# First-half sums kept in tiles of the split sums and of outputs; a third tile each for queries and values, one more of 64-bit words, two more of 32-bit words

## The chip, the cores and the metric

The kernel runs on 1 core of one Trainium2 chip. The metric is the device time of one execution in microseconds (us). A core has five engines that run side by side, each through its own list of instructions in a fixed order: TensorE (PE, matrix products, with PEld for its weight loads), VectorE (DVE), ScalarE (ACT), GpSimd (POOL) and SyncE (SP, which in this kernel issues nearly all DMAs, written SPq in the profile). An instruction whose data or tile is not ready holds up all that stand behind it on its engine.

## The reference

An attention over 4 batches of 12 heads, then two feed-forward blocks on its output:

```python
# q, k, v: (4, 12, 448, 64)
q_n, k_n = rmsnorm(q, g_q), rmsnorm(k, g_k)
attn = softmax(q_n @ k_n.T / sqrt(64));  x = (attn @ v), heads side by side   # 1792 x 768
h = x @ moe_w_in            # 768 -> 2048
g = relu(h) ** 2
x = g @ moe_w_out           # 2048 -> 768
a, b = x @ moe2_w1, x @ moe2_w2          # 768 -> 1024
out = ((a * b) @ moe2_w3) @ moe2_w_out   # 1024 -> 1024 -> 768
```

The weights arrive as 64-bit floating-point numbers, the rest as 32-bit ones.

## The kernel before

**Products in three parts.** Each 32-bit operand of a feed-forward product is split into a high part (`split_hi`, a copy on ACT) and the rest (`split_lo`, a subtraction on POOL or DVE). `mm3` (L262 to L264) sums high x high, high x rest and rest x high.

**Units of weights.** The weights come as units of 128 x 384 or 128 x 512 numbers, in the order of the list `units`. A 64-bit unit passes through five steps: `load_next` brings it by DMA into a `raw64` tile (L180, 4 tiles); `words` turns its high word on ACT (L194) and its low word on POOL (L200, or ACT L198) into parts of a 32-bit number; `join` (L207, DVE) puts them together in a `raw` tile (6 tiles); `store` writes that to memory for the later batches (L215); `split_hi` and `split_lo` make the `hl` pair that the products read (both at helper lines, L106 and L114). A `raw64` tile is free again after its `join`, a `raw` tile after its `split_lo` and its `store`. `advance` writes these steps a few units ahead of use, by `LOAD64_AHEAD`, `WORD_AHEAD` and the like. There are 120 units of 64 bits; all others are loaded as 32-bit numbers straight into `raw` tiles (L183).

**Stages.** While the 12 heads of batch 0 are worked on, the product of w3 and w_out of the second block is made (`gen_w3o`, units of w3t and wo). While the heads of batch 1 are worked on, the two blocks of batch 0 run (`gen_moe`), with the 64-bit units of w_in, w_out, w1 and w2. Batches 2 and 3, and the end, run with stored 32-bit units. The main loop over heads writes one head's attention in pieces (scores L524 and L525, their maximum `nb` L526 and L527, exponentials `p` L543, transposes L570, products with v L622) and between them `fill` steps of the feed-forward products. From head 12 on the exponentials go through a DMA on SP (`pw<-p`, L549) before their transposes.

**Order.** A scheduler then orders each engine's instructions: an instruction is placed as soon as its inputs, its engine and a free tile of its pool are there by the scheduler's own reckoning, earlier ones of the program first. So the number of tiles of a pool decides how far ahead an engine's list runs.

**First-half sums.** The 2048-wide layer is done in two halves. `keep(e)` (L340) copies the sums of the first half of `w_out` into an `acc` tile on ACT, 6 in all; `add(e)` (L346) adds those of the second half on DVE and splits the sum into an `x2` pair (6 tiles).

Of the kernel before, what the change touches and what calls it, by code (L numbers as in the profile page):

```python
# [8 lines left out]
F32 = mybir.dt.float32  # L9
F32R = mybir.dt.float32r  # L10
U16 = mybir.dt.uint16
U32 = mybir.dt.uint32
# [17 lines left out]
def attention_moe_kernel(  # L30
# [16 lines left out]
    B, P, H, C, D = q_nat.shape  # L47
    S = P * C
# [26 lines left out]
    JOIN_AHEAD = 2  # L75
    WORD_AHEAD = 3
    LOAD32_AHEAD = 3
    LOAD64_AHEAD = 5

    const = ctx.enter_context(tc.tile_pool(name="const", bufs=1))  # L80
    xp = ctx.enter_context(tc.tile_pool(name="x", bufs=8))
    actp = ctx.enter_context(tc.tile_pool(name="act", bufs=8))
    x2p = ctx.enter_context(tc.tile_pool(name="x2", bufs=6))
    accp = ctx.enter_context(tc.tile_pool(name="acc", bufs=6))
    rawp = ctx.enter_context(tc.tile_pool(name="raw", bufs=6))
    hlp = ctx.enter_context(tc.tile_pool(name="hl", bufs=4))
    t2 = ctx.enter_context(tc.tile_pool(name="t2", bufs=2))
    t1 = ctx.enter_context(tc.tile_pool(name="t1", bufs=1))
    t3 = ctx.enter_context(tc.tile_pool(name="t3", bufs=3))
# [81 lines left out]
    def is64(i):  # L171
        return units[i][0].dtype != F32

    def load_next():
        i = pos["load"]
        src = units[i][0]
        n = src.shape[-1]
        if is64(i):
            t = t3.tile([128, 512, 2], U32, name="raw64", tag="raw64", bufs=4)
            nc.sync.dma_start(out=t[:, :n, :], in_=src.bitcast(U32).rearrange("p (n t) -> p n t", t=2))  # L180
        else:
            t = rawp.tile([128, 512], F32, name="raw", tag="raw")
            nc.sync.dma_start(out=t[:, :n], in_=src)  # L183
        raws[i] = t
        pos["load"] += 1
# [134 lines left out]
    def gen_moe(b):  # L320
        u = U0 + b * (2 * NFC + 4 * NE + 4 * NJ + 2 * NE)
        x = [xs.pop((b, i)) for i in range(KX)]
        acc = [None] * NE
        x2 = [None] * NE
        for half in range(2):
# [11 lines left out]

            def keep(e):
                def f(ps):
                    acc[e] = accp.tile([128, S], F32, name="acc", tag="acc")  # L340
                    copy_on("a", acc[e], ps)
                return f

# [65 lines left out]
    def load_head(h):  # L409
        if not (0 <= h < NH):  # L410
            return
        b, hh = divmod(h, H)
        t = t2.tile([128, S], F32, name="qt", tag="qt")
        nc.sync.dma_start(out=t, in_=q_t[b, hh])
        qts[h] = t

    def load_v(h):
        if not (0 <= h < NH):
            return
        b, hh = divmod(h, H)  # L420
        t = t2.tile([128, C, D], F32, name="v", tag="v")
        nc.sync.dma_start(out=t, in_=v_in[b, hh])
        vs[h] = t

# [343 lines left out]
```

## Time and profile before

| | |
|---|---|
| median of 3 runs | 1235.23 us (1233.96 to 1238.2) |
| the profiled execution: its time, its span | 1234.55 us, 1232.8 us |
| mean granted TensorE clock | 0.991 |
| busy, us: PE, DVE, ACT, POOL | 1160.9, 709.7, 728.5, 781.3 |
| DMA | 207.63 MB, mean 168 GB/s |

The span is the time from the first to the last instruction. Busy times are unions of an engine's instructions. In rows of instructions, `out<-in` are tiles by the program's names, x is a count, and the bracket gives the engine's idle time before the instruction and what ended it.

### The profile page before, as it was taken

Reading aid. Unit: us, or ns where it says so; the run is one execution under the profiler, and the core shown is the slowest. Engines: PE = TensorE matmul, PEld = TensorE weight load, DVE = VectorE, ACT = ScalarE, POOL = GpSimd, SP = SyncE. Lnnn points to the kernel's source line nnn. Section 1 sums busy time; section 2 is a strip of 40 time slices with the busy share of each in tenths; the row PEclk is TensorE's granted clock in tenths of the full one; section 3 lists DMA queues with packets and bytes.
Section 4 is the critical chain, followed back from the end, with each engine's and each line's share of the span. In section 5 each row is a group of like instructions: output and inputs, shape, how many; then the busy total and the mean of one; then the engine's idle time right before and its main releaser. Section 6 shows DMA issues by size and latency. Waiting matters only on the chain.

```text
span 1232.8 us, 18950 instructions
## 1 busy us (share of the span) xinstructions
PE 1160.9 (94%) x6192; PEld 1049.3 (85%) x6192; DVE 709.7 (58%) x1314; ACT 728.5 (59%) x1553; POOL 781.3 (63%) x772
## 2 busy tenths in 40 slices
PE   3789999998989899999999999999999999999998
PEld 2578888886878789998998998999999999999998
DVE  6699879768978774646567555655664421012100
ACT  5889876767657565656645555656545554343342
POOL 5875534655676655766776764856766556678673
PEclk9999999999998999999999999999999999999999
DMA  7774557888888755555535455544544443333342
GB/s 218 244 238 151 165 146 226 276 283 264 251 264 257 234 180 179 146 148 145 151 118 161 139 169 158 143 142 127 154 123 120 138 138 113 107 116 102 104 125 75
DMA packets 111347, 207.63 MB, mean 168 GB/s; under 512 B 12208, under 2 KB 66704, under 8 KB 111248
## 3 DMA queue, kind: packets, MB, share of 16 engines
q1 hardware_dynamic: 107792, 200.92, 54.0%
q10 hardware_dynamic: 3456, 5.51, 1.2%
q8 instruction: 49, 0.80, 0.3%
q14 instruction: 50, 0.41, 0.1%
HBM read 149.95 MB, written 27.53 MB: 144 GB/s over the span
## 4 chain that ended last, share of the span: by engine, by line
PE 60%; DMA 4%; DVE 2%; POOL 2%; ACT 1%; issue 1%; SPq 0%; DVEq 0%; POOLq 0%; ACTq 0%
PE mm L262 17%; PE mm L263 17%; PE mm L264 17%; PE kv L622 3%; PE pt L570 3%; DMA raw<-w 2%; DMA pw<-p 2%; PE sc L525 1%; PE sc L524 1%; POOL hl L114 1%; DVE raw L207 1%; PE kv L508 1%; PE mm L611 0%; ACT p L543 0%; POOL x L114 0%
## 5 line engine op out<-in xcount | busy, mean ns | idle before, releaser
L114 POOL TENSOR_TENSOR hl<-raw,hl 128x384 fp32r<-128x384 f32 (+1 forms) x383 | 446.4, 1169 | 258.5 <-ACT hl L106 253.3
L106 ACT ACTIVATE hl<-raw 128x384 fp32r<-128x384 f32 (+1 forms) x416 | 233.7, 564 | 147.6 <-PE mm L264 85.6
L263 PE MATMUL mm<-x,hl 128*128 128x448 f32 (+1 forms) x832 | 306.2, 368 | 8.6 <-POOL x L114 8.6
L262 PE MATMUL mm<-x,hl 128*128 128x448 f32 (+1 forms) x832 | 310.5, 373 | 3.8 <-ACT x L106 1.8
L264 PE MATMUL mm<-x,hl 128*128 128x448 f32 (+1 forms) x832 | 305.7, 367 | 4.5 <-POOL hl L114 2.6
L263 PE MATMUL mm<-act,hl 128*128 128x448 f32 (+1 forms) x640 | 234.4, 366 | 3.3 <-POOL act L114 3.2
L262 PE MATMUL mm<-act,hl 128*128 128x448 f32 (+1 forms) x640 | 236.9, 370 | 0.0
L264 PE MATMUL mm<-act,hl 128*128 128x448 f32 (+1 forms) x640 | 233.6, 365 | 0.7 <-DVE hl L114 0.7
L543 ACT ACTIVATE p<-sc,nb,rr 112x448 f32<-112x448 f32 x192 | 137.4, 719 | 86.4 <-DVE nb L527 83.0
L263 PEld LDWEIGHTS mm<-x,hl 128*128 128x128 f32 x832 | 158.1, 190 | 22.1 <-POOL x L114 10.2
L264 PEld LDWEIGHTS mm<-x,hl 128*128 128x128 f32 x832 | 158.2, 190 | 19.0 <-POOL hl L114 4.0
L262 PEld LDWEIGHTS mm<-x,hl 128*128 128x128 f32 x832 | 157.9, 190 | 18.5 <-ACT x L106 3.3
L526 DVE TENSOR_REDUCE nb<-sc 112x1 f32<-112x448 f32 x192 | 113.1, 615 | 35.6 <-PE sc L525 34.3
L263 PEld LDWEIGHTS mm<-act,hl 128*128 128x128 f32 x640 | 121.0, 189 | 14.3 <-POOL act L114 4.8
L264 PEld LDWEIGHTS mm<-act,hl 128*128 128x128 f32 x640 | 120.9, 189 | 10.6 <-DVE hl L114 1.1
L262 PEld LDWEIGHTS mm<-act,hl 128*128 128x128 f32 x640 | 121.0, 189 | 9.4
L114 DVE TENSOR_TENSOR ptr<-pt,ptr 128x448 fp32r<-128x448 f32 x144 | 87.1, 619 | 72.0 <-ACT ptr L106 71.4
L200 POOL TENSOR_SCALAR raw<-raw 128x384 uint32<-128x384 uint16 (+1 forms) x110 | 82.1, 747 | 73.0 <-DMA raw<-w_in 18.8
L207 DVE SCALAR_TENSOR_TENSOR raw<-raw 128x384 uint32<-128x384 uint32 (+1 forms) x120 | 84.8, 711 | 39.8 <-POOL hl L114 25.2
L194 ACT ACTIVATE raw<-raw 128x384 f32<-128x384 f32 (+1 forms) x120 | 70.5, 597 | 53.9 <-DMA raw<-w 18.0
L114 POOL TENSOR_TENSOR act<-gf,act 128x448 fp32r<-128x448 f32 x80 | 97.4, 1218 | 7.2 <-DVE gf L334 3.0
L334 DVE TENSOR_TENSOR gf<-mm,r 128x448 f32<-128x448 f32 x64 | 39.8, 621 | 94.4 <-ACT r L330 93.9
(82 smaller groups left out, 1588.7 us busy)
## 6 DMA issues: line engine op xcount, KB each, us to landing
pw<-p SPq DMA_DIRECT2D x72, 392.0 KB, 4.3
raw<-f_in SPq DMA_DIRECT2D x96, 192.0 KB, 2.4
raw<-f_out SPq DMA_DIRECT2D x72, 256.0 KB, 2.7
raw<-f SPq DMA_DIRECT2D x96, 192.0 KB, 2.4
raw<-w_in SPq DMA_DIRECT2D x32, 384.0 KB, 4.5
raw<-w_out SPq DMA_DIRECT2D x24, 512.0 KB, 6.1
raw<-w SPq DMA_DIRECT2D x32, 384.0 KB, 4.9
raw<-w3o SPq DMA_DIRECT2D x48, 256.0 KB, 2.7
```

The source lines that it names most:

```text
L106: nc.scalar.activation(out=out, in_=in_, func=AF.Copy)
L114: e.tensor_tensor(out=out, in0=in0, in1=in1, op=ALU.subtract)
L194: nc.scalar.activation(out=hi, in_=hi, func=AF.Prelu, scale=2.0**-112, alpha=-(2.0**32))
L200: nc.gpsimd.tensor_scalar(out=t[:, :n, 0], in0=low, scalar1=2.0**-13, scalar2=2.0**-14 - 0.5, op0=ALU.mult, op1=ALU.add)
L207: nc.vector.scalar_tensor_tensor(out=f[:, :n].bitcast(U32), in0=t[:, :n, 1], scalar=3, in1=t[:, :n, 0], op0=ALU.logical_shift_left, op1=AL ...
L262: nc.tensor.matmul(ps, w[:, 0, wk, :], x[0], start=(i == 0), stop=False)
L263: nc.tensor.matmul(ps, w[:, 0, wk, :], x[1], start=False, stop=False)
L264: nc.tensor.matmul(ps, w[:, 1, wk, :], x[0], start=False, stop=(i == last))
L334: nc.vector.tensor_tensor(out=gf, in0=ps, in1=r, op=ALU.mult)
L526: nc.vector.tensor_reduce(out=nb[:, j:j + 1], in_=o[j], axis=AX.X, op=ALU.max, negate=True)
L543: nc.scalar.activation(out=p, in_=o[j], func=AF.Exp, scale=d["rq"][:, c:c + 1], bias=nb[:, j:j + 1], accum_out=sm[:, i, c:c + 1],)
L570: nc.tensor.transpose(to[:kn, c * P:(c + 1) * P], d["p"][c][:, k0:k0 + kn], one)
```

## The change

The pool of `acc` tiles goes. The first-half sums 0 to 3 lie in two `x2` tiles, two sums in each, and the sums 4 and 5 in the two `osb` tiles, which the outputs use as well. The room is given to one more `raw64` tile (5), two more `raw` tiles (8), and a third tile each for `qt` and `v`. `LOAD64_AHEAD` is 6 in place of 5, so a 64-bit load is written one unit earlier.

```diff
--- before.py
+++ after.py
@@ -75,14 +75,13 @@
     JOIN_AHEAD = 2
     WORD_AHEAD = 3
     LOAD32_AHEAD = 3
-    LOAD64_AHEAD = 5
+    LOAD64_AHEAD = 6
 
     const = ctx.enter_context(tc.tile_pool(name="const", bufs=1))
     xp = ctx.enter_context(tc.tile_pool(name="x", bufs=8))
     actp = ctx.enter_context(tc.tile_pool(name="act", bufs=8))
     x2p = ctx.enter_context(tc.tile_pool(name="x2", bufs=6))
-    accp = ctx.enter_context(tc.tile_pool(name="acc", bufs=6))
-    rawp = ctx.enter_context(tc.tile_pool(name="raw", bufs=6))
+    rawp = ctx.enter_context(tc.tile_pool(name="raw", bufs=8))
     hlp = ctx.enter_context(tc.tile_pool(name="hl", bufs=4))
     t2 = ctx.enter_context(tc.tile_pool(name="t2", bufs=2))
     t1 = ctx.enter_context(tc.tile_pool(name="t1", bufs=1))
@@ -176,7 +175,7 @@
         src = units[i][0]
         n = src.shape[-1]
         if is64(i):
-            t = t3.tile([128, 512, 2], U32, name="raw64", tag="raw64", bufs=4)
+            t = t3.tile([128, 512, 2], U32, name="raw64", tag="raw64", bufs=5)
             nc.sync.dma_start(out=t[:, :n, :], in_=src.bitcast(U32).rearrange("p (n t) -> p n t", t=2))
         else:
             t = rawp.tile([128, 512], F32, name="raw", tag="raw")
@@ -337,7 +336,11 @@
 
             def keep(e):
                 def f(ps):
-                    acc[e] = accp.tile([128, S], F32, name="acc", tag="acc")
+                    if e >= 4:
+                        acc[e] = t2.tile([128, S], F32, name="osb", tag="osb")
+                    elif e % 2 == 0:
+                        pair = x2p.tile([128, 2, S], F32, name="acc", tag="x2")
+                        acc[e], acc[e + 1] = pair[:, 0, :], pair[:, 1, :]
                     copy_on("a", acc[e], ps)
                 return f
 
@@ -410,7 +413,7 @@
         if not (0 <= h < NH):
             return
         b, hh = divmod(h, H)
-        t = t2.tile([128, S], F32, name="qt", tag="qt")
+        t = t2.tile([128, S], F32, name="qt", tag="qt", bufs=3)
         nc.sync.dma_start(out=t, in_=q_t[b, hh])
         qts[h] = t
 
@@ -418,7 +421,7 @@
         if not (0 <= h < NH):
             return
         b, hh = divmod(h, H)
-        t = t2.tile([128, C, D], F32, name="v", tag="v")
+        t = t2.tile([128, C, D], F32, name="v", tag="v", bufs=3)
         nc.sync.dma_start(out=t, in_=v_in[b, hh])
         vs[h] = t
 
```

No instruction is added or taken away. The lists of the engines change in the following places. Line numbers of the change are 3 higher behind its `keep`, and 1 lower ahead of it.

DVE in the second half of the stage of batch 0's blocks, from the two transposes `ptr` ahead of a head's last scores to their maxima `nb`; the joins are the rows `raw<-raw64`, and a tile's number in the change is two or three lower than in the kernel before. Before:

```order
L114 TENSOR_TENSOR ptr_2969<-pt_2964,ptr_2969 128x448
L207 SCALAR_TENSOR_TENSOR raw_3094<-raw64_2980 128x512
L114 TENSOR_TENSOR hl_2987<-raw_2935,hl_2987 128x512
L207 SCALAR_TENSOR_TENSOR raw_3119<-raw64_3009 128x512
L207 SCALAR_TENSOR_TENSOR raw_3151<-raw64_3055 128x512
L114 TENSOR_TENSOR khl_3458<-kx_3456,khl_3458 112x4x64
L114 TENSOR_TENSOR ptr_3040<-pt_3035,ptr_3040 128x448
L114 TENSOR_TENSOR pte_3047<-pt_3042,pte_3047 64x448
L207 SCALAR_TENSOR_TENSOR raw_3215<-raw64_3089 128x384
L207 SCALAR_TENSOR_TENSOR raw_3257<-raw64_3114 128x384
L526 TENSOR_REDUCE nb_3079<-sc_3080 112x1
L526 TENSOR_REDUCE nb_3079<-sc_3084 112x1
```

The same place of the change:

```order
L113 TENSOR_TENSOR ptr_2968<-pt_2963,ptr_2968 128x448
L206 SCALAR_TENSOR_TENSOR raw_3212<-raw64_3053 128x384
L113 TENSOR_TENSOR hl_2986<-raw_2934,hl_2986 128x512
L206 SCALAR_TENSOR_TENSOR raw_3254<-raw64_3087 128x384
L206 SCALAR_TENSOR_TENSOR raw_3284<-raw64_3112 128x384
L113 TENSOR_TENSOR khl_3455<-kx_3453,khl_3455 112x4x64
L113 TENSOR_TENSOR ptr_3039<-pt_3034,ptr_3039 128x448
L113 TENSOR_TENSOR pte_3046<-pt_3041,pte_3046 64x448
L206 SCALAR_TENSOR_TENSOR raw_3306<-raw64_3144 128x384
L529 TENSOR_REDUCE nb_3077<-sc_3078 112x1
L529 TENSOR_REDUCE nb_3077<-sc_3082 112x1
```

Between the same attention rows stand joins of later units: where the join into raw_3151 stood right ahead of `khl`, now stands that into raw_3284 (raw_3287 of before), and raw_3306 (3309 of before) stands ahead of the maxima in place of raw_3257.

POOL at the same place, with the low words (`raw64<-raw64`) of the units that DVE joins there. The number of a `raw64` tile is that of its place of loading, which lies one unit earlier in the change: by the join rows, raw64_3008 is now the unit of raw_3149, which was raw64_3055 before. Before:

```order
L200 TENSOR_SCALAR raw64_2980<-raw64_2980 128x512
L114 TENSOR_TENSOR x_2954<-xf_2580,x_2954 128x448
L200 TENSOR_SCALAR raw64_3009<-raw64_3009 128x512
L114 TENSOR_TENSOR hl_3016<-raw_2985,hl_3016 128x512
L200 TENSOR_SCALAR raw64_3055<-raw64_3055 128x512
L108 TENSOR_SCALAR khl_3458<-kx_3456 112x4x64
L480 TENSOR_TENSOR kx_3769<-kn_2168,rr_2585 112x256
```

Of the change:

```order
L199 TENSOR_SCALAR raw64_3087<-raw64_3087 128x384
L113 TENSOR_TENSOR x_2953<-xf_2579,x_2953 128x448
L199 TENSOR_SCALAR raw64_3112<-raw64_3112 128x384
L113 TENSOR_TENSOR hl_3015<-raw_2984,hl_3015 128x512
L199 TENSOR_SCALAR raw64_3144<-raw64_3144 128x384
L107 TENSOR_SCALAR khl_3455<-kx_3453 112x4x64
L483 TENSOR_TENSOR kx_3766<-kn_2167,rr_2584 112x256
```

Before, the low word of the unit that DVE joins ahead of `khl` (raw64_3055) was POOL's last row ahead of its own `khl`; now that unit's low word (raw64_3112) stands two rows earlier, and the last one (raw64_3144) is joined only behind DVE's `khl`, `ptr` and `pte`.

SP from the third to the fourth DMA of exponentials (`pw<-p`) of batch 1; `raw<-w_in` and `raw<-w_out` are loads of 64-bit units. Before:

```order
L549 DMA pw<-p 112x896
L180 DMA raw_2626<-w_in 128x768
L215 DMA f_in<-raw 128x384
L180 DMA raw_2645<-w_out 128x1024
L215 DMA f_in<-raw 128x384
L180 DMA raw_2692<-w_out 128x1024
L414 DMA qt<-q_t 128x448
L549 DMA pw<-p 112x896
```

Of the change:

```order
L552 DMA pw<-p 112x896
L214 DMA f_in<-raw 128x384
L179 DMA raw_2691<-w_out 128x1024
L214 DMA f_in<-raw 128x384
L179 DMA raw_2715<-w_out 128x1024
L214 DMA f_in<-raw 128x384
L179 DMA raw_2763<-w_out 128x1024
L214 DMA f_in<-raw 128x384
L417 DMA qt<-q_t 128x448
L552 DMA pw<-p 112x896
```

There are three unit loads between the two DMAs in both lists, but they are three units further on: the first two loads of w_out, which stood here, are issued ahead of the third `pw<-p`. Of the DMAs of exponentials 6 to 20, each stands behind three or four more unit loads than before.

PE near the start, from the second scores of head 1 on (the rows `mm` are products of `gen_w3o`, three for each wo unit, which is an `act` tile here). Before:

```order
L525 MATMUL sc_446<-kt_353,ql_203 112x448
L570 MATMUL pt_482<-ident_103,p_417 128x112
L570 MATMUL pt_489<-ident_103,p_417 128x112
L262 MATMUL mm_226<-act_306,hl_290 128x384
L263 MATMUL mm_226<-act_306,hl_290 128x384
L264 MATMUL mm_226<-act_306,hl_290 128x384
L524 MATMUL sc_450<-kt_353,qh_202 112x448
L525 MATMUL sc_450<-kt_353,ql_203 112x448
L570 MATMUL pt_482<-ident_103,p_417 128x112
L570 MATMUL pt_489<-ident_103,p_417 128x112
L262 MATMUL mm_226<-act_318,hl_290 128x384
```

Of the change:

```order
L573 MATMUL pt_481<-ident_100,p_416 128x112
L573 MATMUL pt_488<-ident_100,p_416 128x112
L261 MATMUL mm_223<-act_305,hl_289 128x384
L262 MATMUL mm_223<-act_305,hl_289 128x384
L263 MATMUL mm_223<-act_305,hl_289 128x384
L261 MATMUL mm_223<-act_317,hl_289 128x384
L262 MATMUL mm_223<-act_317,hl_289 128x384
L263 MATMUL mm_223<-act_317,hl_289 128x384
L261 MATMUL mm_223<-act_332,hl_289 128x384
L262 MATMUL mm_223<-act_332,hl_289 128x384
L263 MATMUL mm_223<-act_332,hl_289 128x384
L527 MATMUL sc_449<-kt_352,qh_199 112x448
```

Two groups of three products have moved ahead of the scores sc_449 (sc_450 of before). Further on, 63 in place of 48 products stand ahead of the first scores of head 2; from that head's second half on the counts differ by 6 at most, and from head 11 on by none. The order of the products and the attention on PE is then the same.

## Rows read from the trace of the kernel before

**Rows 1.** Busy time by stretch: us, each engine (count), PEclk, DMA share, GB/s.

```profile
0.00:60.00 60.00, 30.32 (x115) 21.55 (x116) 39.29 (x89) 39.63 (x82) 42.36 (x52) 0.97 0.74 231
60.00:210.00 150.00, 138.66 (x838) 124.58 (x837) 136.36 (x279) 123.59 (x270) 80.10 (x98) 1.00 0.61 182
210.00:450.00 240.00, 214.57 (x1109) 189.91 (x1108) 190.86 (x338) 153.94 (x335) 150.47 (x161) 0.96 0.81 256
450.00:1232.80 782.80, 777.40 (x4135) 713.25 (x4133) 343.13 (x612) 411.31 (x869) 508.38 (x463) 1.00 0.45 134
```

**Rows 2.** Waits of PE from 210 to 450 us: total, times, longest.

```profile
PE sc L524 <- ACT p L543: 8.8, 8, 2.4
PE pt L570 <- DMA pw<-p: 6.2, 5, 2.1
```

**Rows 3.** Waits of DVE from 210 to 450 us.

```profile
DVE raw L207 <- POOL hl L114: 22.5, 16, 2.8
...
DVE raw L207 <- POOL raw L200: 6.2, 6, 2.7
...
DVE raw L207 <- DMA raw<-w_in: 1.8, 1, 1.8
```

**Rows 4.** Timeline of DVE from 246 to 259 us.

```profile
248.03 0.69 DVE L207 SCALAR_TENSOR_TENSOR raw<-raw 128x512 uint32<-128x512 uint32 x1 [2.70 <-POOL raw L200]
...
253.16 0.56 DVE L207 SCALAR_TENSOR_TENSOR raw<-raw 128x384 uint32<-128x384 uint32 x1 [1.81 <-DMA raw<-w_in]
253.64 1.15 DVE L526 TENSOR_REDUCE nb<-sc 112x1 f32<-112x448 f32 x2
```

**Rows 5.** Timeline of POOL from 243 to 256 us.

```profile
243.93 0.67 POOL L200 TENSOR_SCALAR raw<-raw 128x512 uint32<-128x512 uint16 x1 [1.74 <-DMA raw<-w_out]
...
247.33 0.64 POOL L200 TENSOR_SCALAR raw<-raw 128x512 uint32<-128x512 uint16 x1 [0.52 <-DMA raw<-w_out]
...
252.59 3.19 POOL L200 TENSOR_SCALAR raw<-raw 128x384 uint32<-128x384 uint16 x3
```

**Rows 6.** Timelines of ACT and of PE from 254 to 259 us.

```profile
255.81 0.72 ACT L543 ACTIVATE p<-sc,nb,rr 112x448 f32<-112x448 f32 x1 [3.23 <-DVE nb L527]
...
256.68 0.46 PE L524 MATMUL sc<-kt,qh 128*112 128x448 f32 x1 [0.46 <-ACT p L543]
...
258.34 0.46 PE L524 MATMUL sc<-kt,qh 128*112 128x448 f32 x1 [1.00 <-ACT p L543]
```

**Rows 7.** Timelines of DVE and of PE from 350 to 362 us.

```profile
351.38 0.56 DVE L207 SCALAR_TENSOR_TENSOR raw<-raw 128x384 uint32<-128x384 uint32 x1 [1.88 <-POOL raw L200]
...
354.62 0.47 PE L264 MATMUL mm<-act,hl 128*128 128x448 f32 x1 [0.73 <-DVE hl L114]
359.56 0.46 PE L524 MATMUL sc<-kt,qh 128*112 128x448 f32 x1 [2.44 <-ACT p L543]
```

**Rows 8.** Busy time of the stretch right behind it, columns as in group 1.

```profile
361.40:364.90 3.50, 3.50 (x11) 3.12 (x10) 3.28 (x11) 1.06 (x3) 1.28 (x3) 0.51 0.93 226
```

**Rows 9.** Timeline of SP's DMA issues, 222 to 234 and 251 to 260 us.

```profile
231.26 0.33 SPq L414 DMA_DIRECT2D qt<-q_t  x1
231.69 0.37 SPq L180 DMA_DIRECT2D raw<-w_out  x1
...
257.23 0.33 SPq L414 DMA_DIRECT2D qt<-q_t  x1
258.31 0.52 SPq L549 DMA_DIRECT2D pw<-p  x1
```

**Rows 10.** Busy time by stretch near the start, columns as in group 1.

```profile
26.00:56.00 30.00, 19.29 (x74) 14.26 (x75) 19.82 (x32) 22.43 (x50) 25.95 (x26) 0.94 0.77 242
56.00:120.00 64.00, 56.88 (x343) 50.24 (x341) 61.38 (x117) 57.13 (x121) 43.73 (x50) 1.00 0.63 197
```

**Rows 11.** Timeline of PE from 34 to 60 us.

```profile
36.43 0.36 PE L524 MATMUL sc<-kt,qh 128*112 128x448 f32 x1
...
56.19 0.43 PE L524 MATMUL sc<-kt,qh 128*112 128x448 f32 x1
```

## The prediction

> **What bounds the kernel now.** I read busy times by stretch first. From 450 us to the end PE is busy for 777.4 of 782.8 us [rows 1]: there the products stand one behind the other, and tiles can give back no more than the missing 5.4 us. All else that can be won lies ahead of that: 29.7 us without PE work in the first 60, 11.3 from 60 to 210, and 25.4 from 210 to 450, the stage that turns 64-bit units into words. That last stage also has a mean granted clock of 0.96. In it no engine is full (DVE 190.9 of 240 us, the DMA engines 0.81), so PE waits for things that are late and not for things that are too many. The waits of PE say for what: 8.8 us for exponentials to leave the score tiles, 6.2 us for the DMA of exponentials [rows 2]. The waits of DVE say why exponentials are late: its list holds joins (L207) among the maxima, and they wait 22.5 us in 16 cases for POOL's split of an older unit, that is for a `raw` tile to come free, and 8.0 us in 7 cases for the unit's own words (6.2 named so, and 1.8 named after a DMA, of which more below) [rows 3].
>
> Two places show the chain whole. At 248.03 a join starts after 2.70 us of waiting for POOL's low word, at 253.16 another after 1.81 [rows 4]; POOL made that second word among the three from 252.59 on, so the row's DMA is a misnomer [rows 5]. The maxima follow at once, at 253.64. ACT's exponential starts at 255.81 after 3.23 idle, and PE loses 0.46 and 1.00 us [rows 6]. At 351.38 a join has waited 1.88 for a low word, and behind it on DVE stand a split and maxima: PE loses 0.73 and 2.44 us [rows 7], and the 3.50 us behind those run at a granted clock of 0.51, the lower level of 1.2 GHz [rows 8].
>
> **What the change does, part by part.** It adds no instruction, so every term is one of order and of waiting.
>
> *More `raw` and `raw64` tiles.* The order shows what the scheduler makes of them. Loads and words stand three units further on between the same attention rows, joins two units further on, and the splits and products where they were. From this three things follow.
>
> First, a join that waits for a `raw` tile is not helped. With 6 tiles the join of unit k takes the tile of unit k-6; with 8 tiles there now stands the join of unit k+2, which takes the tile of unit k+2-8, the same one, and POOL's split of it stands where it stood. The 22.5 us of DVE remain. At this point the Trainium skill speaks for more: "Perfetto Trace Analysis", Identifying Performance Opportunities, says that gaps that repeat on the engine that should be saturated can mean too little SBUF for the next tile, in count or size. The 16 waits look just so; by the page alone the stage would lose its 25.4 us of gaps and the sum would be 1209 us. The order speaks against this here, since the list runs ahead by as many units as it gets tiles.
>
> Second, the same holds of loads against words: both moved by three units, so ACT and POOL wait for a landing where they waited before.
>
> Third, words moved by one unit more than joins. This is the one slack that the change makes. At the place of 248.03 the join's low word now stands two rows earlier on POOL, which in the old run is the word that was done at 244.60 (243.93 + 0.67) against 247.97 [rows 5]; the 2.70 us go. At 253.16 the same: the word was made ahead of POOL's `khl`. So the 8.0 us of the 7 waits go. What PE has of it: the 0.46 and 1.00 at the first place entirely, since 4.51 us of DVE's waiting stand ahead of maxima that were 3.23 us late; at the second at most the join's own 1.88 of the 3.17 us lost there. That is 3.34 us. If the gap at 359.56 shrinks the clock may stay up; 3.50 us at half speed cost 1.75. Together 5.1 us. From below the bound is nothing: some other row of the same DVE list could be late in the join's stead. From above it is the whole wait for exponentials, 8.8, with the clock, 10.5. I take 5, since the two places are traced link by link.
>
> *A third tile for queries and for values.* At 257.23 SP issues a query load that had waited for its tile at the head of SP's list, but 1.08 us later, at 258.31, comes the DMA of exponentials that waits for ACT anyway, and no unit load stands between [rows 9]. Of the six waits of this kind in the stage only the one that ends at 231.26 has a unit load, at 231.69, between the two. I take nothing; if the exponentials came earlier, the query would have been next in line to block, so here the third tile is cover for the first term and is worth a part of it, not more. For values I find no hole that PE feels, and take nothing.
>
> *First-half sums in other tiles.* The copies of `keep` and the additions of `add` remain. The pair tiles hold two of six `x2` tiles; the fifth split sum needs the first pair's tile, whose second sum was split off two products of 24 triples earlier. The `osb` tiles are idle between the outputs of one batch and those of the next. So I cost it at nothing. Without that cover it would be a wait inside the last 782.8 us, in which PE has no room: each microsecond would count in full.
>
> *The start.* Here the order of PE and DVE themselves changes: wo units come first, attention later. 63 products in place of 48 stand ahead of head 2's first scores, which started at 56.19, and two groups ahead of head 1's second ones, at 36.43 [rows 11]. From 26 to 56 us POOL, with 25.95 of 30, paces the wo units, and from 56 to 120 DVE, with 61.38 of 64, is the bound [rows 10]. So what attention loses ahead of 56 us cannot be made up on DVE behind it, and what the wo units win counts only where POOL's 4.05 us of idle time close up. The 15 products are 2.8 us of PE (777.4 us for 4135 instructions are 0.19 each [rows 1]). Between 4 us won and about 6 lost (three wo units at two POOL instructions each, of 25.95 / 26 = 1.0 us) I take 1 us lost.
>
> *Three units sooner in and out.* The stage of 210 to 450 has 25.4 us of gaps for the 88 units of w_in, w_out, w1 and w2, 0.29 us a unit: three units fewer give back 0.9. They are worked in the 150 us ahead of it, where DVE is busy for 136.4 [rows 1]: there three joins of 0.69 us [rows 4] cost up to 2.1. I take nothing, with both ends kept.
>
> **The sum.** 1234.55 (the profiled execution's time, 0.7 below the median of 1235.23) - 5.0 for the word slack + 1.0 for the start + 0 for the rest gives 1230.5 us, 0.4% under the median. What I call no change is within 0.3%, 3.7 us, about what a measurement of this kernel can tell: 1231.5 to 1238.9.
>
> **Rivals.** *Nothing comes of it* (0.24): the pipeline is only relabelled, the joins that no longer wait for words wait for tiles instead, behind the same POOL list, and the DMAs of exponentials stay where they are. For this speaks that 22.5 of the 30.5 us of join waits are for tiles; against it the two traced places. About 1234.5 us.
>
> *The waits for tiles go too* (0.13): each join that starts sooner lets SP load sooner and POOL split sooner, and the stage closes up on its own. Then the 8.8 us of waits for exponentials, the 0.73 us and a clock step (1.75) go, and half of the 6.2 us for the DMA, which is issued earlier: 14.4 in all, 1220 us. The page of the Trainium skill named above would have it so; by the order its chance is small.
>
> *The start loses more than the stage wins* (0.18): head 2's first scores come at 60 us or later, 4 us late, DVE has no room to make it up until 120, and the three extra joins ahead of 210 us add to it. At 6 us lost and 1 won it ends at 1239.5, slower than before. It decides from about 58 us for those scores: then the loss is over 2 us and eats the smaller bound of the gain.
>
> **How the numbers follow.** The forecast holds 0.45. Its own range is 1226 to 1233, so a fifth of it (0.09) lies inside the band of no change. Faster: 0.13 + 0.36 = 0.49. No change: 0.24 + 0.09 = 0.33. Slower: 0.18. The range goes from 1220, the case in which the tile waits go too, to 1239; it leaves out a part of the slow case above (0.10) and some 0.08 below.
>
> **What would show it right or wrong.** In the profile of the changed kernel: waits of L207 for POOL L200 and for DMAs from 210 to 450 us near zero in place of 8.0, those for POOL L114 near 22.5 (if they fall below 12, the second rival is right); PE's wait for exponentials there 4 to 5 us; waits of L194 and L200 for landings within a fifth of what they are; PE's idle time ahead of 60 us 29 to 33; head 2's first scores at 55 to 58 us; PE from 450 us on as full as it was. The forecast is wrong if PE's gaps from 210 to 450 us do not shrink although the word waits are gone, or if the first 120 us hold the difference.

## The result and the profile after

The changed kernel takes 1242.12 us (median of 10 runs, 1239.26 to 1247.28), where the kernel before took 1235.6 beside it (10 runs, 1232.86 to 1238.2). The ratio is 1.0056, with a 95% interval of 1.0042 to 1.0069: slower by 0.56%, some 6.9 us. The profiled execution took 1239.59 us with a span of 1237.6, so it lies 2.5 us under the median; that of the kernel before (1234.55) lies 1 us under the 1235.6.

Busy time by stretch, in the columns of [rows 1]:

```profile
0.00:60.00 60.00, 30.06 (x101) 22.23 (x102) 38.67 (x85) 37.98 (x78) 44.14 (x51) 0.89 0.77 241
60.00:210.00 150.00, 134.28 (x813) 120.97 (x812) 133.76 (x270) 120.46 (x263) 81.98 (x96) 0.99 0.63 183
210.00:450.00 240.00, 216.68 (x1126) 190.33 (x1125) 200.82 (x347) 155.06 (x338) 157.65 (x160) 0.98 0.80 253
450.00:1237.60 787.60, 781.89 (x4157) 717.33 (x4156) 345.81 (x614) 414.94 (x878) 512.02 (x466) 1.00 0.45 133
```

Against [rows 1] the largest difference lies in the second line. From 60 to 210 us PE did 134.28 us of work in place of 138.66, and 25 instructions fewer are recorded. The first line is 14 instructions behind as well (101 for 115), of which more below. The third line moved the other way (216.68 for 214.57), and the last one has gaps of 5.7 us where it had 5.4. A cut inside the second line places the loss; the first row is of the kernel before, the second of the changed one:

```profile
97.00:165.00 68.00, 64.31 (x397) 58.03 (x395) 60.17 (x133) 57.80 (x129) 34.36 (x44) 1.00 0.52 155
```

```profile
97.00:165.00 68.00, 59.16 (x357) 53.56 (x356) 61.58 (x123) 54.37 (x118) 38.66 (x45) 0.97 0.57 166
```

PE has 40 instructions fewer in the same 68 us. DVE was busy for longer (61.58 for 60.17) with ten instructions fewer, so they took more time on average; POOL took 38.66 us for 45 instructions, before 34.36 for 44. What PE waited for from 97 to 170 us, first before, then after:

```profile
PE sc L524 <- ACT p L543: 2.7, 3, 1.3
PE pt L570 <- DVE ptr L114: 0.4, 1, 0.4
```

```profile
PE sc L527 <- ACT p L546: 4.5, 4, 1.8
PE pt L573 <- DVE ptr L113: 2.9, 2, 2.5
```

The first scores of the heads, read from PE's timeline, say the same: head 2 starts 6.2 us late (62.4 for 56.2), head 5 0.2 late (97.4 for 97.2), head 11 8.1 late (172.5 for 164.4), head 15 10.2 late (240.1 for 229.9), head 24, where the full stage begins, 4.6 late (467.3 for 462.7). Head 2's row, beside [rows 11]:

```profile
62.44 0.36 PE L527 MATMUL sc<-kt,qh 128*112 128x448 f32 x1
```

So the start's delay is gone by head 5, 8 us are lost while heads 5 to 11 run and 2 more up to head 15, and 5.6 come back from there to head 24. Such times come from one profiled execution of each kernel: in the eight kernels of this text whose order on PE is that of the kernel before up to head 5, head 5 starts between 97.2 and 99.3 us, so a difference of one or two us between two profiles says little.

One place shows how a late head comes about. Timelines of the changed kernel, first DVE, then POOL, ACT and PE:

```profile
121.91 0.68 DVE L499 SCALAR_TENSOR_TENSOR ql<-qt,gg,qh 128x448 fp32r<-128x448 f32 x1
122.50 1.81 DVE L530 TENSOR_TENSOR nb<-nb,rr 112x2 f32<-112x2 f32 x1
```

```profile
121.80 1.26 POOL L483 TENSOR_TENSOR kx<-kn,rr 112x256 f32<-112x256 f32 x1
123.02 1.27 POOL L113 TENSOR_TENSOR hl<-raw,hl 128x512 fp32r<-128x512 f32 x1
```

```profile
124.34 0.73 ACT L546 ACTIVATE p<-sc,nb,rr 112x448 f32<-112x448 f32 x1 [1.67 <-DVE nb L530]
```

```profile
125.21 0.45 PE L527 MATMUL sc<-kt,qh 128*112 128x448 f32 x1 [1.41 <-ACT p L546]
```

The maxima's last step (`nb`, two columns) took 1.81 us and ended at 124.31, just behind POOL's split, which ended at 124.29. ACT's exponential waited 1.67 us for it, and PE 1.41 for the exponential. At 158.47 PE lost another 2.52 us to a `ptr` of 157.72. On DVE there stood ahead of it a step of 1.23 us beside a POOL split of 1.29, a join, and a `khl` that waited 1.00 us for POOL and took 1.34:

```profile
153.53 1.23 DVE L436 SCALAR_TENSOR_TENSOR nt<-nt,ss 112x32 f32<-112x32 f32 x1
```

```profile
153.42 1.29 POOL L113 TENSOR_TENSOR hl<-raw,hl 128x512 fp32r<-128x512 f32 x1 [3.93 <-ACT hl L105]
```

The waits of DVE and of PE from 210 to 450 us, beside [rows 2, 3]:

```profile
DVE raw L206 <- POOL hl L113: 19.5, 15, 2.5
...
DVE raw L206 <- DMA raw<-w_in: 1.2, 1, 1.2
DVE raw L206 <- DMA raw<-w: 1.2, 1, 1.2
```

```profile
PE sc L527 <- ACT p L546: 8.6, 8, 2.4
PE pt L573 <- DMA pw<-p: 7.1, 6, 3.0
```

The joins' waits for words fell from 8.0 to 2.4 us (forecast: near zero). PE's waits for exponentials did not follow: 8.6 for 8.8, where 4 to 5 had been forecast. Of that stage two DVE groups by line and shape show what else moved; the first fence is of before, the second of after:

```profile
L207 DVE SCALAR_TENSOR_TENSOR raw<-raw 128x512 uint32<-128x512 uint32 x24 | 18.4, 773 | 7.8 <-POOL raw L200 3.8 <-POOL hl L114 3.6 <-ACT raw L194 0.3
...
L527 DVE TENSOR_TENSOR nb<-nb,rr 112x2 f32<-112x2 f32 x19 | 6.8, 359 | 0.1
```

```profile
L206 DVE SCALAR_TENSOR_TENSOR raw<-raw 128x512 uint32<-128x512 uint32 x24 | 19.0, 799 | 0.7 <-POOL hl L113 0.7
...
L530 DVE TENSOR_TENSOR nb<-nb,rr 112x2 f32<-112x2 f32 x20 | 9.9, 497 | 0.1
```

The wide joins stopped waiting (7.8 us to 0.7), and DVE's busy time in the stage went from 190.86 to 200.82 us: nine more instructions, and longer ones, the two-column `nb` among them. Part of that is the cut by time, since all heads run later. Cut at the first scores of heads 11 and 24 instead, the joins' waits fell from 34.0 to 25.1 us, DVE was busy for 245.2 us (437 instructions) in place of 241.7 (440), and PE's gaps went from 29.6 to 27.5; in `sums_only`, the first run below, which has no more tiles than the kernel before, they are 27.2.

### The profile page after: what moved, and what is told of

Same layout as the page of the kernel before. It is cut to its first block, busy times and chain, and to the rows that moved or that the text cites. A ratio compares the mean times of both kernels' runs of the same rounds, so it can differ in the third digit from the quotient of the medians.

```text
span 1237.6 us, 18953 instructions
## 1 busy us (share of the span) xinstructions
PE 1162.9 (94%) x6192; PEld 1050.8 (85%) x6192; DVE 719.1 (58%) x1314; ACT 728.4 (59%) x1553; POOL 795.8 (64%) x772
## 4 chain that ended last, share of the span: by engine, by line
PE 65%; DVE 12%; DMA 9%; POOL 5%; ACT 4%; issue 4%; SPq 1%; DVEq 0%; ACTq 0%; POOLq 0%
PE mm L261 18%; PE mm L263 18%; PE mm L262 18%; PE kv L625 3%; PE pt L573 3%; DMA pw<-p 3%; DMA raw<-w 2%; DVE raw L206 2%; DVE nb L529 2%; PE sc L527 2%; PE sc L528 2%; POOL hl L113 1%; ACT p L546 1%; DMA raw<-w_in 1%; POOL raw L199 1%
## 5 line engine op out<-in xcount | busy, mean ns | idle before, releaser
L529 DVE TENSOR_REDUCE nb<-sc 112x1 f32<-112x448 f32 x192 | 113.4, 615 | 34.2 <-PE sc L528 32.9
L199 POOL TENSOR_SCALAR raw<-raw 128x384 uint32<-128x384 uint16 (+1 forms) x110 | 90.0, 818 | 67.0 <-DMA raw<-w_in 18.9
L206 DVE SCALAR_TENSOR_TENSOR raw<-raw 128x384 uint32<-128x384 uint32 (+1 forms) x120 | 83.2, 697 | 34.1 <-POOL hl L113 22.5
L113 POOL TENSOR_TENSOR act<-gf,act 128x448 fp32r<-128x448 f32 x80 | 97.6, 1221 | 6.9 <-DVE gf L333 3.0
L193 ACT ACTIVATE raw<-raw 128x384 f32<-128x384 f32 (+1 forms) x120 | 70.0, 597 | 49.0 <-DMA raw<-w 22.9
L527 PE MATMUL sc<-kt,qh 128*112 128x448 f32 x192 | 75.2, 392 | 21.6 <-ACT p L546 19.1
```

The lines of the kernel that those rows point to most:

```text
L113: e.tensor_tensor(out=out, in0=in0, in1=in1, op=ALU.subtract)
L193: nc.scalar.activation(out=hi, in_=hi, func=AF.Prelu, scale=2.0**-112, alpha=-(2.0**32))
L199: nc.gpsimd.tensor_scalar(out=t[:, :n, 0], in0=low, scalar1=2.0**-13, scalar2=2.0**-14 - 0.5, op0=ALU.mult, op1=ALU.add)
L206: nc.vector.scalar_tensor_tensor(out=f[:, :n].bitcast(U32), in0=t[:, :n, 1], scalar=3, in1=t[:, :n, 0], op0=ALU.logical_shift_left, op1=AL ...
L527: nc.tensor.matmul(o[j], d["qh"][:, c * P:(c + 1) * P], d["kt"], start=True, stop=False)
L529: nc.vector.tensor_reduce(out=nb[:, j:j + 1], in_=o[j], axis=AX.X, op=ALU.max, negate=True)
```

## The experiments

Two theories stood first. **Run-ahead**: more tiles let joins and words of `w_in` move into the stretch of 60 to 165 us, where DVE has no room. **Start**: the other order of wo units and of heads 1 and 2 costs the time, by itself. Beside them stood the two other parts of the change, the query and value tiles and the sums. Ratios are to the kernel before, which ran beside each (medians 1236.0 to 1237.3 us), with 95% intervals.

**The parts one by one.** `sums_only` has the moved sums and all other numbers as before; the others keep one or two parts more:

```diff
 no_third_qv: the changed kernel with
-        t = t2.tile([128, S], F32, name="qt", tag="qt", bufs=3)
+        t = t2.tile([128, S], F32, name="qt", tag="qt")
-        t = t2.tile([128, C, D], F32, name="v", tag="v", bufs=3)
+        t = t2.tile([128, C, D], F32, name="v", tag="v")
 raw8_only: these, and
-    LOAD64_AHEAD = 6
+    LOAD64_AHEAD = 5
-            t = t3.tile([128, 512, 2], U32, name="raw64", tag="raw64", bufs=5)
+            t = t3.tile([128, 512, 2], U32, name="raw64", tag="raw64", bufs=4)
 raw64_only: no_third_qv, and
-    rawp = ctx.enter_context(tc.tile_pool(name="raw", bufs=8))
+    rawp = ctx.enter_context(tc.tile_pool(name="raw", bufs=6))
 sums_only: all of these
```

sums_only: 

> Only the first-half sums move into the x2 and osb tiles; all other tiles are as before, and no engine's order changes but that of a few DVE, ACT and POOL rows near the sums. Run-ahead theory (more 32-bit tiles pull joins and words into the stage of 60 to 210 us, where DVE is nearly full): 0, within 1.5 us of before. Start theory (the other order of wo units and heads 1 and 2 costs the time): 0. Queries theory (the third qt and v tiles cost it): 0. Sums theory (an x2 or osb tile is waited for in the last 782.8 us): +4 us or more, and PE gaps behind 450 us.

raw8_only: 

> The sums move, and the 32-bit raw tiles are 8; raw64 stays at 4, loads run 5 ahead, qt and v have two tiles. Loads, words and joins then stand two units further on from about head 11, and heads 1 and 2 start as before. Run-ahead theory: two more joins ahead of 210 us, +4 to +6 us by 165 us, little given back: 1239 to 1241. Start theory: no loss, within 1.5 us of before. Queries theory: within 1.5 us of before. The word slack of the prediction is not made here (words and joins move alike), so the 8.0 us of DVE's waits for words stay.

raw64_only: 

> The sums move, raw64 has 5 tiles and loads run 6 ahead; raw stays at 6, qt and v have two tiles. The start takes the order of the changed kernel (63 products ahead of head 2's first scores); words stand one unit further on and joins where they were. Run-ahead theory: no extra joins ahead of 210 us, so no loss there, and the word slack pays: 1231 to 1234. Start theory: +5 us by 165 us, less 3 in the stage: 1237 to 1239. Queries theory: 1231 to 1234.

no_third_qv: 

> The changed kernel with qt and v back at two tiles each. PE's order is the same as that of the changed kernel; SP's and DVE's differ. Run-ahead theory: as slow as the changed kernel, 1240 to 1244. Start theory: the same, 1240 to 1244. Queries theory: the loss from 97 to 165 us is gone, 1231 to 1235.

Measured: sums_only 1.0001 (0.9985 to 1.0017), so no cost of the sums can be seen. raw8_only 1.0017 (1.0002 to 1.0032), raw64_only 1.0073 (1.0053 to 1.0093), no_third_qv 1.0086 (1.0065 to 1.0107). The fifth 64-bit tile with the loads six ahead brings a loss of its own, against the run-ahead theory as I had put it (no extra joins, so no loss) and more than the start theory had for it. The queries theory falls: without the third tiles the kernel is no faster, and rather slower (the two intervals just overlap). In raw8_only, which has the start of the kernel before and two more joins ahead of head 11, that head comes at 171.9 us, 6.3 behind that of sums_only (165.6), as the run-ahead theory has it; but the time, 1237.9 us, is under its 1239 to 1241: most of the delay is made up later. In raw64_only the word waits of 210 to 450 us are gone, and the tile waits are longer than in [rows 3]:

```profile
DVE raw L206 <- POOL hl L113: 27.8, 18, 3.5
```

In this kernel (raw64_only) one pulled join is seen at work. DVE first, then POOL:

```profile
117.32 1.21 DVE L455 TENSOR_REDUCE ss<-qn 112x16 f32<-112x1024 f32 x1
123.78 0.56 DVE L206 SCALAR_TENSOR_TENSOR raw<-raw 128x384 uint32<-128x384 uint32 x1 [5.25 <-POOL hl L113]
124.25 0.62 DVE L113 TENSOR_TENSOR ptr<-pt,ptr 128x448 fp32r<-128x448 f32 x1
```

```profile
121.91 0.61 POOL L483 TENSOR_TENSOR kx<-kn,rr 112x256 f32<-112x256 f32 x1
122.48 1.26 POOL L113 TENSOR_TENSOR hl<-raw,hl 128x512 fp32r<-128x512 f32 x1
```

The join wants the tile that the split of 122.48 frees, and POOL made that split behind the keys of three heads. The `ptr` behind the join was late, and PE lost 3.04 us:

```profile
124.92 0.47 PE L625 MATMUL kv<-ptr,vhl 128*128 128x448 f32 x1 [3.04 <-DVE ptr L113]
```

**Joins held back, the third tiles alone, and tiles that come late.** A hold orders the join of a given unit behind a given row of maxima on DVE (`maxima` lists the instructions of L529 in the order of the program, and `HELD` gives the unit and the place in that list); it adds an order on that engine and no work:

```diff
     def join(i):
...
+        behind = ExitStack()
+        if i in HELD:
+            behind.enter_context(tc.issue_after(maxima[HELD[i] - 1]))
         nc.vector.scalar_tensor_tensor(
...
+        behind.close()
 joins_held: changed kernel; raw64_held: raw64_only; both with
+    HELD = {33: 30, 34: 32, 35: 34, 36: 38, 37: 40, 38: 44, 39: 46, 40: 50, 41: 52, 42: 54, 43: 54, 44: 54}
 qv_only: sums_only, with
+        t = t2.tile([128, S], F32, name="qt", tag="qt", bufs=3)
+        t = t2.tile([128, C, D], F32, name="v", tag="v", bufs=3)
 late_tiles: no_third_qv, with
+            extra = i >= 44 and i % 5 == 0
+            tag, n64 = ("raw64x", 1) if extra else ("raw64", 4)
...
+        extra = i >= 44 and i % 4 == 0
+        return rawp.tile([128, 512], F32, name="raw", tag="rawx" if extra else "raw", bufs=2 if extra else 6)
...
-            for k in range(pos["load"], min(i + LOAD64_AHEAD, NU - 1) + 1):
+            for k in range(pos["load"], min(i + (LOAD64_AHEAD if i >= 39 else 5), NU - 1) + 1):
```

joins_held: 

> The changed kernel, with the joins of units 33 to 44 held behind the maxima they stood behind in the kernel before (by their order on DVE alone; nothing waits that did not). Start and tiles are those of the changed kernel. Run-ahead theory (joins pulled forward into the stage of 60 to 165 us, where DVE is nearly full, cost the time): head 11's first scores at 166 to 169 us in place of 172.5, and 1236 to 1239 us where before has 1236. Start theory (the order of wo units ahead of heads 1 and 2 costs it): head 11 stays at 171 to 174 us, 1241 to 1244.

raw64_held: 

> The run with 5 raw64 tiles alone, with the same joins held as they stood before. In the run without the hold a join at 123.78 us waited 5.25 us on DVE for POOL's split of an older unit, four maxima earlier than where the kernel before has it, and PE lost 3.04 us behind it. Run-ahead theory: that wait goes, head 11's first scores come at 167 to 170 us in place of 172.5, and the time falls from a ratio of 1.007 to 1.001 to 1.004. Start theory: the ratio stays at 1.006 to 1.009.

qv_only: 

> The sums move and qt and v have three tiles; raw stays at 6, raw64 at 4, loads run 5 ahead. The order at the start changes again (70 products ahead of head 2's first scores, where before has 48 and the changed kernel 63), and the joins of w_in in the stage of 60 to 165 us stand where they did but for one. Run-ahead theory: no loss, 1234 to 1238 us. Start theory: another order of wo units costs as much as the changed one did: 1240 to 1244.

late_tiles: 

> The extra raw64 tile, the two extra raw tiles and the loads 6 ahead are used from unit 44 on (the unit that is joined at about 200 us), qt and v have two tiles. PE's order up to head 12 and the joins up to there are those of the kernel before. Both theories lay the loss ahead of 165 us: head 11's first scores within 1.5 us of 165, and the whole within 1.5 us of before or faster by up to 4 us (1232 to 1237.5), the more the more of the word slack PE can use. If the loss comes from the stage of 210 to 450 us after all: 1240 or more. The prediction's word slack by itself: 5 us faster.

joins_held: 1.0017 (1.0002 to 1.0032), head 11 at 169.4 us. With the start of the changed kernel and its tiles, the joins alone put back give 0.39% or 4.8 us; head 11 came 0.4 us behind the range of the run-ahead theory and the time inside it. But of the 8 us lost from head 5 to head 11 only 3 came back: that stretch takes 71.8 us here, 75.1 in the changed kernel and 67.2 in the kernel before. raw64_held: 1.0047 (1.0029 to 1.0065). The wait of 5.25 us is gone, but head 11 came at 172.1, hardly sooner, so that wait was not what delayed it; the ratio lies between the two theories. qv_only: 1.0085 (1.0061 to 1.0109). Third query and value tiles alone, with no more joins ahead, cost about as much as the whole change, or more (the intervals overlap): head 2 at 65.3, head 5 4.6 us late, head 11 10.6 late. The 4.6 us are as the start theory has it; the 6.0 behind head 5 are named by neither theory. late_tiles: 1.0004 (0.9990 to 1.0018), head 11 at 166.4. It has the word slack without what was pulled ahead. Its waits from 210 to 450 us:

```profile
DVE raw L212 <- POOL hl L113: 21.3, 16, 2.5
...
DVE raw L212 <- POOL raw L205: 2.5, 2, 2.1
```

```profile
PE sc L533 <- ACT p L552: 8.2, 8, 1.7
PE pt L579 <- DMA pw<-p: 7.7, 4, 2.9
```

Word waits 2.5 us, and 0.6 in one named after a DMA, for 8.0; PE's waits for exponentials 8.2 for 8.8, and no time won: the word slack, by itself, is worth nothing that can be told here.

**A dose of joins, and joins held further.**

```diff
 joins_twice: sums_only, with
+        for _ in range(2 if 33 <= i <= 40 else 1):
             nc.vector.scalar_tensor_tensor(
 before_joins_later: sums_only; changed_joins_later: changed kernel; late_joins_later: late_tiles; all three with
+    HELD = {33: 36, 34: 40, 35: 44, 36: 46, 37: 48, 38: 50, 39: 52, 40: 52, 41: 54}
```

joins_twice: 

> The kernel before with the sums moved, and the joins of units 33 to 40 done twice into the same tile: eight more DVE instructions of 0.55 to 0.7 us between 110 and 200 us, five of them ahead of head 11, with no more tiles, loads or words. Theory that DVE paces the stage of 56 to 172 us: each comes in full, head 11 at 167.5 to 170 us and the whole at +3 to +6 us (ratio 1.0025 to 1.005). Theory that a pulled join costs only by its waits for POOL: within 1.5 us of before.

before_joins_later: 

> The kernel before with the sums moved, and the joins of units 33 to 41 held two to three units behind where they stood: three joins fewer ahead of head 11. Theory that DVE paces the stage: head 11's first scores 1.5 to 3 us sooner (162.5 to 164.5); the whole 1 to 3 us faster (ratio 0.9975 to 0.9992) if the stage of 210 to 450 us doesn't take it back, 0 if it does. Theory that only waits of pulled joins cost: no change at head 11, since those joins waited 0.2 us there.

changed_joins_later: 

> The changed kernel with joins held still further back than in the run with the joins of before: three fewer ahead of head 11 than there. Theory that DVE paces the stage: 1 to 3 us faster than that run, a ratio of 0.999 to 1.001. If the later stage takes it back: 1.0017 again.

late_joins_later: 

> The tiles used from unit 44 on, as in the run with late tiles, and the joins of units 33 to 41 held back as in the run of before with later joins. If the two add up: 1 to 4 us faster than before (ratio 0.997 to 0.9992), and the only version here ahead of both kernels; if the word slack is worth nothing and the later stage takes the rest back: within 1.5 us of before.

joins_twice: 1.0024 (1.0013 to 1.0035), 3.0 us for eight joins of about 0.6, head 11 at 167.5, 1.9 behind that of sums_only with five of the eight ahead of it. Some three fifths of the added time come through: DVE nearly paces this stretch, not wholly. changed_joins_later: 0.9989 (0.9975 to 1.0002), 8.3 us under the changed kernel's ratio and level with before. Head 11 comes at 168.8 and head 24 at 460.1 us, so of the 7.2 us by which head 24 is sooner than in the changed kernel 3.7 are won ahead of head 11 and 3.5 behind it (the profiled executions lie 2.9 and 2.5 us under the medians of the two kernels). before_joins_later: 1.0019 (1.0009 to 1.0030), with three joins fewer ahead and head 11 at 169.5, 3.9 us later than in sums_only. That refutes the plain form of the theory, that fewer joins in the stretch are better. late_joins_later: 1.0038 (1.0023 to 1.0053), against both expectations. From 97 to 165 us changed_joins_later reads:

```profile
97.00:165.00 68.00, 61.48 (x380) 56.27 (x379) 57.53 (x121) 54.71 (x120) 33.44 (x42) 0.97 0.43 126
```

DVE is down by 4.05 us for two instructions fewer than in the changed kernel, POOL by 5.22 for three, and PE got through 23 instructions more.

**The same hold on three further bases**, with the `HELD` of the last three:

```diff
 no_third_qv_later: no_third_qv, raw8_later: raw8_only, qv_later: qv_only; each with
+    HELD = {33: 36, 34: 40, 35: 44, 36: 46, 37: 48, 38: 50, 39: 52, 40: 52, 41: 54}
```

no_third_qv_later: 

> The changed kernel with two tiles each for queries and values (ratio 1.0086 without a hold), and the joins of units 33 to 41 held as in the changed kernel with later joins (0.9989). PE's and DVE's joins stand as there. Theory that pulled joins cost in the changed start: most of it goes, 1.001 to 1.004. Theory that the third query and value tiles are what makes the held version good: 1.005 or more.

raw8_later: 

> Eight raw tiles alone (1.0017 without a hold, start as in the kernel before), with the same hold. If holding joins helps wherever they were pulled ahead: 0.998 to 1.000. If it costs wherever the start is that of the kernel before, as it did there (1.0019): 1.002 to 1.004.

qv_later: 

> Third tiles for queries and values alone (1.0085 without a hold; 70 products ahead of head 2's first scores), with the same hold: three joins fewer ahead of head 11. If the loss there is the start's (head 5 was 4.6 us late): head 5 stays 4 to 5 us late and the ratio at 1.006 to 1.010. If the stage of 97 to 165 us gives back what the joins take: 1.003 to 1.006.

| kernel | without hold | with the later hold |
|---|---|---|
| changed | 1.0056 | 0.9989 (0.9975 to 1.0002) |
| no_third_qv | 1.0086 | 1.0019 (1.0001 to 1.0037) |
| qv_only | 1.0085 | 1.0054 (1.0034 to 1.0074) |
| raw8_only | 1.0017 | 1.0010 (0.9995 to 1.0024) |
| sums_only | 1.0001 | 1.0019 (1.0009 to 1.0030) |
| late_tiles | 1.0004 | 1.0038 (1.0023 to 1.0053) |

The hold gives 0.67% on both kernels that have all raw tiles from the start, 0.31% with the third query and value tiles alone, where the intervals overlap (head 5 stays 5.0 us late there, so the start's share remains), nothing that can be told with eight raw tiles and the old start, between what the two theories said, and it costs where joins had not been pulled (with sums_only the intervals overlap, with late_tiles they do not). In the time of the whole program pulled joins are a clear cost only together with the changed start. With the start of the kernel before they delay head 11 too (raw8_only), but only 0.17% of it is left at the end. The third query and value tiles give 0.3% where the raw tiles are many (1.0086 to 1.0056, and 1.0019 to 0.9989), and cost 0.84% where they are few.

**A rival that these runs leave open: PE's own order.** The joins are not all that moves. Between the first scores of heads 5 and 11 PE has the order of the kernel before in sums_only and late_tiles alone, and these two take 67.4 and 67.2 us for it, as the kernel before does (67.2). The other fourteen kernels have nine other orders there, in which products, scores and transposes change places (with the changed start four products more stand there too), and take 68.8 (joins_twice) to 75.7 us (no_third_qv); kernels that share an order lie within 0.9 us of one another. No run moves joins and keeps PE's order, so how much is the joins' and how much that order's is not shown.

## Why the prediction was wrong, by its own steps

**What bounds the kernel.** The reading of the last 782.8 us held. That of 60 to 210 us was too short: I saw 11.3 us of gaps to win there, and that DVE was busy for 136.4 of 150 [rows 1], and priced the joins that come into it at 2.1 us at most. That is where most of the loss is.

**Tile waits stay.** Right for the changed kernel: 19.5 us in 15 cases for 22.5 in 16, where "near 22.5" had been forecast. The reason given for it, that the join of unit k+2 takes the same tile as unit k did, is too strong: in raw8_only, with two more tiles and joins two units further on, these waits fell to 12.8 us in 11 cases (and 2.9 in one named after a DMA of values), and PE's gaps stayed at 24.6 us. The rule of the Trainium skill, "Perfetto Trace Analysis", Identifying Performance Opportunities, that repeated gaps can mean too few tiles, is not borne out here: with eight and five tiles for six and four the stage's gaps went from 25.4 to 23.3 us only.

**Loads against words.** Right: ACT's waits for landings in words went from 42.3 to 37.1 us (18.0, 12.2, 12.1 to 22.9, 6.1, 8.1), and POOL's from 39.1 to 32.9, both within a fifth.

**The word slack, -5 us.** Failed. The order made it and the waits went (8.0 to 2.4), but the step from there to PE did not hold. I had added up PE's gaps behind two places where a join stood late, and taken the maxima to move up by what the joins no longer waited. In the trace after, the waits of all joins together fell by 9.2 us (22.5 + 6.2 + 1.8 + 0.6 to 19.5 + 1.2 + 1.2) and DVE's busy time in the same 240 us rose by 10.0, some of it work that had moved into them; in raw64_only they fell by 3.1 only, since 5.3 us came back as tile waits, which was the first rival. late_tiles shows the term nearly alone, with the extra tiles tied to fixed units: 1.0004, between a gain of 1.2 and a loss of 2.2 us, where 5 were forecast.

**Third query and value tiles, 0.** Failed. I looked from 210 us on, and the effect is ahead of that: with the changed start head 5 begins at 96.7 to 97.6 us in the three kernels that have the third tiles and at 99.1 to 101.9 in the four that have two. Its sign hangs on what else stands in the lists.

**Sums, 0.** Right: 1.0001 (0.9985 to 1.0017).

**The start, +1.** For the changed kernel right as far as head 5: 29.9 us of PE idle ahead of 60 us, inside 29 to 33, and head 5 0.2 us late with four products fewer ahead of it, 0.8 at the 0.19 us each of the prediction. But head 2 came at 62.4, past the 58 us from which the third rival was to decide, so that sign was badly chosen: head 2 is no measure of the loss, since heads 2 to 5 made it up. In qv_only they did not. Whether the changed start goes on costing time behind head 5 is open: with the joins put back heads 5 to 11 still take 71.8 and 71.3 us (joins_held, raw64_held), for 67.2 before.

**Three units sooner, 0 (-0.9 to +2.1).** Failed: this term was mis-sized, and with the word slack it is what made the sum wrong. I priced the pulled joins by their own 0.69 us, as three joins ahead of 210 us, though the order shown ahead of the prediction has joins only two units further on: in the trace after, 41 joins stand on DVE ahead of head 11's maxima for 39. joins_held gives 4.8 us back and changed_joins_later 8.3. The joins' own time is the smaller part: by joins_twice, 1.9 us at head 11 for five joins, two joins are worth about 0.8 us there, an estimate. The rest is argued from single places of the traces: a pulled join holds up what stands behind it on DVE, its words share POOL with the keys of later heads and with the splits that free tiles, and DVE and POOL lengthen one another's instructions. What each of these is worth, and what PE's changed order is, no run shows. The third rival came nearest in time (1239.5), with three joins ahead of 210 us named in it, but put most of the loss at the start.

**What stays open.** Why holding three joins back costs 0.18% in sums_only and 0.34% with late tiles, why heads 5 to 11 still take 4 us more than before with the joins put back, and why pulled joins cost more at the end of the run with the changed start. Open is also what changed_joins_later wins behind head 11: from 210 to 450 us PE waited 10.2 us for exponentials in it and 2.7 for their DMA (before 8.8 and 6.2), so it is not the way that the prediction had for the word slack. The runs separate the parts, but each is also another order of the same lists, PE's among them. No version beat both kernels by more than its interval: changed_joins_later is faster than the changed one by 0.67%, and level with before.

## What to carry to other kernels

A wait that goes away need not be a gain: here the joins' waits fell by 8.9 us between heads 11 and 24 and PE's gaps ended where they were in sums_only (27.5 and 27.2 us). Read busy time and waits of an engine as one sum, before and after, over the same work and not over the same time. Where a scheduler fills its lists greedily, more tiles also move work into an earlier stage, so find out from the order which stage receives it, and price it there by what stands behind it too, not by its own duration alone. Parts of a change that only reorder don't add up (third tiles: +0.84% alone, -0.3% beside the others), so try them together and apart. And when a version changes one list, compare the others before naming the cause.

## What the runs showed of the hardware

DVE instructions that read two small operands took many times as long beside POOL. The step `nb` of two columns stands 96 times in each of the seventeen traces. Where no POOL instruction ran at the same time it took 0.14 to 0.16 us in all of them; beside one it took up to 2.47 (the kernel before, at 666.45). In the changed kernel it took 1.81 us at 122.50, and elsewhere:

```profile
151.70 0.15 DVE L530 TENSOR_TENSOR nb<-nb,rr 112x2 f32<-112x2 f32 x1
```

The long one ended 0.02 us behind the POOL split that ran beside it. The Trainium skill, "SBUF — State Buffer", Who interferes with whom, says that a DVE instruction with two inputs in SBUF contends with a GpSimd instruction that reads SBUF, and that the port pair they share is an exclusive lock. The trace agrees at 153.53, where the `nt` of 1.23 us ended at 154.76 and POOL's split, begun first, at 154.71. At 122.50 the `nb` stood longer than that: it began while POOL made a `kx`, which ended at 123.06, and it also stood behind the split that POOL began at 123.02.

Over the program DVE's busy time rose by 9.4 us (709.65 to 719.06), of which 4.7 are `nb` (35.3 to 40.0), and POOL's by 14.5 (781.32 to 795.79) for the same work. So the effect is in the kernel before as well, and how much of it a kernel gets depends on which instructions happen to meet. I had priced each engine's instructions by their means before, as if they were fixed.

The clock moved too: the profiled execution of the changed kernel has two stretches of 6.8 us near the start at a granted clock of 0.50, the lower level of 1.2 GHz.

```profile
38.00:44.80 6.80, 4.88 (x16) 3.84 (x15) 3.85 (x7) 2.68 (x7) 6.34 (x6) 0.50 0.61 182
48.30:55.10 6.80, 5.72 (x18) 5.03 (x18) 4.48 (x8) 6.37 (x15) 6.39 (x7) 0.50 1.02 345
```

PE was busy for 4.88 and 5.72 of these 6.8 us; from 28 to 38 us, ahead of the first, it was busy for 4.99 of 10 at a clock of 1.00. They do not belong to the changed start as such: with the same order on PE up to head 5, no_third_qv and raw64_held show a clock of 1.00 over the first 60 us, and sums_only, with the order of the kernel before, 0.91. What they cost no run shows by itself; head 5 was 0.2 us late behind them. A third such stretch, 3.4 us at 113.1, lies where the 8 us are lost; joins_held has none between heads 5 and 11 (clock 1.00) and takes 71.8 us for them, so a part of the 3.3 us that it wins there may be the clock's.
